# List-scheduled attention-and-GLU block: a longer assumed latency for DMA transposes, an earlier place for the gate-times-up products, a slack for TensorE

## The chip, the core and the metric

One core of a Trainium2 chip. The metric is device time in microseconds (us). A run is called slow when it is over 1.5% above the fastest of its kernel; one run of the kernel before (249.89 us) is such a run and is left out.

## The reference

For 2048 tokens of width 512, in bfloat16:

```python
xn  = layernorm(x)
q, k, v = split(xn @ wqkv)                       # 32 heads of 16
phi(a)  = concat(softmax(a @ w_phi), softmax(-(a @ w_phi)))
kv, z   = sum_s phi(k) v, sum_s phi(k)           # per head
A   = (phi(q) kv / (phi(q) z + 1e-6)) @ wo       # linear attention
B   = (gelu(xn @ w_gate) * (xn @ w_up)) @ w_down # width 1376
out = x + A + B
```

## The kernel before

The kernel records every operation with the buffers that it reads and writes, its engine, an assumed cost and (for a DMA) an assumed latency. A list scheduler then simulates the engines with these numbers and so fixes the order of instructions on each. The numbers reach the chip in no other way: **they only decide the order** and, for a few copies that two engines can do, the engine. Each engine is given its instructions in that order, with semaphore waits between them.

```python
def schedule(self):
    ...
    h = min((x for x in cand[n] if x.ready <= t + 1e-9), key=lambda x: x.prio)
    ...
    free[n] = t + h.cost
    h.end = t + h.cost + h.lat
    if h.kb:
        h.end = moved = max(moved, t + h.lat) + h.kb / 345
    for u in h.users:
        slack = self.slack if u.eng == "pe" and n != "pe" else 0.0   # self.slack = 0.0
        u.ready = max(u.ready, ... h.end + slack)
```

The work falls into four stages: a start (layer norm of the first four 128-token tiles, their transposes on TensorE, the first gate matmuls); the gate/up matmuls of the first 512 tokens (L550) with the weight folding; the key, query and value projections (L443, L498); and from about 76 us a long mixed stage. In that stage every attention tile t goes through this chain across engines:

```python
def q_prep(t):                       # POOL sums, VectorE normalises Eq, then two DMA transposes
    ...
    for h in range(2):
        dma("sp", lambda e, h=h: e.dma_start_transpose(EqT[:, t % NQT, 4*h:4*h+4, :], E[...]),
            reads=B_Eq[t], writes=[B_EqT[t % NQT][h]], cost=1.2, lat=1.4, kb=310)

def att(t):                          # TensorE: 2 x 4 small matmuls (L573), VectorE: divide
    ...
    dma("sp", lambda e: e.dma_start_transpose(oT[:, t % NOT, :, :], o_sb[:, k, :]),
        reads=[B_o[k]], writes=[B_oT[t % NOT]], cost=1.2, lat=1.4, kb=310)

def outp(t, b, direct):              # TensorE: 4 matmuls with oT (L594), 11 with hT (L598)
    ...

def ffn(J):                          # 4 gate matmuls, 4 up matmuls (L550), in banks J%2 and 2+J%2
    lin(wg_sb, ...); lin(wu_sb, ...)
    return glu(J, gb, ub)            # ScalarE gelu(gate) -> gs, VectorE hT = gs * up
```

All transposes and all output stores are issued from one queue, SyncE, in order. Gate and up matmuls are the filling with which TensorE covers the chain's latencies. Two PSUM banks each hold gates and ups, so filling is limited by how soon gelu and product free them.

The softmax here doesn't subtract the row's maximum and nothing guards it: scores larger than these inputs give would overflow.

## Time and profile before

| | before |
|---|---|
| median time | 195.86 us (fast runs 195.78 to 195.86) |
| span in the profile | 194.0 us |
| TensorE busy | 187.2 us, 96% |
| VectorE / POOL / ScalarE busy | 64% / 56% / 44% |

The page of the kernel before: busy time per engine, TensorE's share of each fortieth of the span in tenths, and the chain that ended last by engine and line.

```profile
span 194.0 us, 3172 instructions
PE 187.2 (96%) x1175; PEld 95.5 (49%) x1196; DVE 123.6 (64%) x227; ACT 85.3 (44%) x147; POOL 108.3 (56%) x151
...
PE   7999999999999999999899999999999999999993
...
PE 89%; DMA 6%; DVE 2%; issue 1%; ACTq 0%; SPq 0%
```

A digit 9 is 90% or more. TensorE is full except for the first slice, the last, and one dent near the middle. (1175 matmul records beside 1196 weight loads show that 21 matmul records are missing.)

The waits of TensorE in the kernel before: who waited for whom, us in total, times, longest.

```profile
PE ps_all L656 <- DVE warm L390: 1.2, 1, 1.2
PE ps_all L594 <- DMA oT<-o_sb: 0.9, 1, 0.9
PE ps_all L565 <- DMA wg_sb<-in_B_w_gate_dram: 0.3, 1, 0.3
PE ps_all L573 <- DMA EqT<-Eq: 0.2, 1, 0.2
```

The dent itself, from TensorE's timeline of the kernel before. The columns are start, length, what, how many, and in brackets the idle time before it.

```profile
90.47 0.29 PE L573 MATMUL ps_all<-kvr,EqT 128*128 128x68 bf16 x4
90.94 0.30 PE L573 MATMUL ps_all<-kvr,EqT 128*128 128x68 bf16 x4 [0.17 <-DMA EqT<-Eq]
91.07 1.02 PE L550 MATMUL ps_all<-xnT,wu_sb 128*128 128x512 bf16 x4
91.94 1.03 PE L550 MATMUL ps_all<-xnT,wg_sb 128*96 128x512 bf16 x4
92.80 0.42 PE L573 MATMUL ps_all<-kvr,EqT 128*128 128x68 bf16 x8
94.14 1.04 PE L594 MATMUL ps_all<-wo_sb,oT 128*128 128x512 bf16 x4 [0.93 <-DMA oT<-o_sb]
```

The same stretch in the chain of waits of the kernel before shows the two landings (start, us, what):

```profile
86.48 4.41 DMA EqT<-Eq
...
91.63 2.47 DMA oT<-o_sb
```

### The profile page before, as it was taken

How to read it: one execution, taken by the hardware profiler on the slowest of the kernel's cores; microseconds unless marked ns; L12 is line 12 of the kernel's file. 1: busy time of each engine (PE TensorE's matmuls, PEld its weight loads, DVE VectorE, ACT ScalarE, POOL GpSimd, SP SyncE). 2: the span in 40 equal slices, each digit the busy share in tenths (PEclk: the TensorE clock that was granted, in tenths of full speed). 3: DMA queues.
4: the chain of work that ended last, by engine and by line, in shares of the span. 5: the costliest groups of instructions: out<-in, count | busy, mean ns of one | idle time of the engine just before them, and what ended most of it. 6: DMA issues, size and time to landing. Idle time of an engine off the chain costs nothing.

```text
span 194.0 us, 3172 instructions
## 1 busy us (share of the span) xinstructions
PE 187.2 (96%) x1175; PEld 95.5 (49%) x1196; DVE 123.6 (64%) x227; ACT 85.3 (44%) x147; POOL 108.3 (56%) x151
## 2 busy tenths in 40 slices
PE   7999999999999999999899999999999999999993
PEld 2665565444545554454444444444544444454452
DVE  4699895489877675995948987659445361431121
ACT  2382798998797888423040041322223222231000
POOL 6630202799999999999449999979502202021000
PEclk9999999999999999999999999999999999999999
DMA  5999944456020000017456446535442221210101
GB/s 138 349 397 381 189 86 54 83 146 254 3 54 0 3 0 0 0 27 82 91 101 136 84 111 124 107 74 121 92 108 56 55 54 27 54 30 27 54 27 54
DMA packets 41630, 18.60 MB, mean 96 GB/s; under 512 B 33312, under 2 KB 41136, under 8 KB 41616
## 3 DMA queue, kind: packets, MB, share of 16 engines
q1 hardware_dynamic: 40496, 15.94, 35.3%
q0 software_dynamic: 560, 1.95, 3.0%
q10 hardware_dynamic: 560, 0.52, 0.8%
q8 instruction: 9, 0.15, 0.3%
q14 instruction: 5, 0.04, 0.1%
HBM read 8.44 MB, written 2.10 MB: 54 GB/s over the span
## 4 chain that ended last, share of the span: by engine, by line
PE 89%; DMA 6%; DVE 2%; issue 1%; ACTq 0%; SPq 0%
PE ps_all L550 33%; PE ps_all L598 19%; PE ps_all L443 14%; PE ps_all L498 7%; PE ps_all L594 6%; DMA wg_sb<-in_B_w_gate_dram 3%; DMA EqT<-Eq 2%; PE ps_all L565 2%; PE ps_all L573 2%; PE ps_all L518 2%; DMA oT<-o_sb 1%; PE ps_all L624 1%; PE ps_all L636 1%; PE ps_all L647 1%; DVE Eq L480 1%
## 5 line engine op out<-in xcount | busy, mean ns | idle before, releaser
L550 PE MATMUL ps_all<-xnT,wu_sb 128*128 128x512 bf16 (+1 forms) x172 | 43.8, 379 | 0.3
L543 DVE TENSOR_TENSOR hT<-gs,ps_all 128x512 bf16<-128x512 bf16 (+1 forms) x44 | 29.4, 680 | 22.1 <-PE ps_all L550 21.4
L473 POOL TENSOR_TENSOR st<-st 128x256 f32<-128x256 f32 (+1 forms) x54 | 38.9, 720 | 3.7
L541 ACT ACTIVATE gs<-ps_all 128x512 bf16<-128x512 f32 (+1 forms) x44 | 25.8, 597 | 32.6 <-PE ps_all L550 29.6
L550 PE MATMUL ps_all<-xnT,wg_sb 128*128 128x512 bf16 (+1 forms) x154 | 39.8, 379 | 0.3
L598 PE MATMUL ps_all<-wd_sb,hT 128*128 128x512 bf16 (+1 forms) x164 | 38.0, 379 | 0.2
L610 POOL TENSOR_TENSOR ob<-y_sb,x_all 128x512 bf16<-128x512 f32 x12 | 14.7, 1228 | 41.1 <-ACT y_sb L608 41.0
L608 ACT ACTIVATE y_sb<-ps_all 128x512 f32<-128x512 f32 x12 | 7.2, 597 | 45.4 <-PE ps_all L598 40.5
L550 PEld LDWEIGHTS ps_all<-xnT,wu_sb 128*128 128x128 bf16 (+1 forms) x176 | 17.3, 100 | 19.3
L598 PEld LDWEIGHTS ps_all<-wd_sb,hT 128*128 128x128 bf16 (+1 forms) x165 | 16.1, 98 | 19.5
L550 PEld LDWEIGHTS ps_all<-xnT,wg_sb 128*128 128x128 bf16 (+1 forms) x160 | 14.9, 100 | 14.4
L447 ACT ACTIVATE Ek<-ps_all 128x512 bf16<-128x512 f32 x32 | 17.3, 622 | 4.4 <-PE ps_all L443 4.1
L447 ACT ACTIVATE Eq<-ps_all 128x512 bf16<-128x512 f32 x32 | 18.3, 631 | 1.0 <-PE ps_all L443 0.8
L473 POOL TENSOR_TENSOR st<-Eq 128x512 f32<-128x512 bf16 x15 | 17.3, 1155 | 0.0
L473 POOL TENSOR_TENSOR st<-Ek 128x512 f32<-128x512 bf16 x12 | 14.4, 1197 | 3.7 <-ACT Ek L447 3.7
L498 PE MATMUL ps_all<-wv_sb,xnT 128*128 128x512 bf16 x63 | 16.2, 379 | 0.1
L443 PE MATMUL ps_all<-wk,xnT 128*128 128x512 bf16 x62 | 15.8, 379 | 0.1
L443 PE MATMUL ps_all<-wq,xnT 128*128 128x512 bf16 x61 | 15.8, 379 | 0.2
L594 PE MATMUL ps_all<-wo_sb,oT 128*128 128x512 bf16 x56 | 14.7, 379 | 1.0 <-DMA oT<-o_sb 0.9
L480 DVE TENSOR_TENSOR Ek<-Ek,rk 128x1024 bf16<-128x1024 bf16 x16 | 14.0, 875 | 0.5
L480 DVE TENSOR_TENSOR Eq<-Eq,rq 128x1024 bf16<-128x1024 bf16 x16 | 13.0, 812 | 0.4
L406 DVE BATCH_NORM_STATS2 stats<-x_all 128x6 f32<-128x512 bf16 x16 | 10.8, 674 | 1.1 <-DMA x_all<-in_A_x_dram 1.0
(73 smaller groups left out, 191.2 us busy)
## 6 DMA issues: line engine op xcount, KB each, us to landing
out_dram<-ob SPq DMA_DIRECT2D x15, 128.0 KB, 1.9
x_all<-in_A_x_dram SPq DMA_DIRECT2D x3, 512.0 KB, 9.0
wd_sb<-in_B_w_down_dram POOLq DMA_DIRECT2D x1, 1280.0 KB, 8.0
wg_sb<-in_B_w_gate_dram SPq DMA_DIRECT2D x2, 432.0 KB, 6.3
wu_sb<-in_B_w_up_dram SPq DMA_DIRECT2D x2, 432.0 KB, 7.3
wu_sb<-in_B_w_up_dram SPq DMA_DIRECT2D x2, 256.0 KB, 4.6
hT<-in_A_wqkv_dram SPq DMA_DIRECT2D x2, 256.0 KB, 8.2
Eq<-in_A_wqkv_dram SPq DMA_DIRECT2D x2, 256.0 KB, 9.0
```

The lines of the kernel that those rows point to most:

```text
L406: op("dve", lambda e: e.bn_stats(stats[:, t, :], x_all[:, t, :]), reads=[B_x[t]], writes=[B_stats[t]], cost=0.69, extra=extra)
L443: op("pe", [lambda e, i=i: e.matmul(bank(b), xnT[:, i, t * P:(t + 1) * P], w2[:, i, :], start=(i == 0), stop=(i == 3)) for i in range(4)], ...
L447: exps.append(op("act", lambda e, sig=sig: e.activation(E[:, t, :, sig, :], bank(b).rearrange("p (b c) -> p b c", c=64), ACTF.Exp, scale=( ...
L473: op("pool", lambda e, o=o, a=a, n=n: e.tensor_tensor(o, a[:, :, 0:n], a[:, :, n:2 * n], op=ALU.add), reads=ba, writes=bo, cost=c, lock=k < 3)
L480: op("dve", lambda e: e.tensor_tensor(ev, ev, r, op=ALU.mult), reads=[Br], writes=BE, cost=0.92, lock=True)
L498: op("pe", [lambda e, i=i: e.matmul(bank(b), xnT[:, i, t * P:(t + 1) * P], wv_sb[:, i, :], start=(i == 0), stop=(i == 3)) for i in range(4 ...
L541: h = op("act", lambda e: e.activation(gs[0:w, k, :], bank(gb)[0:w, :], ACTF.Gelu_apprx_tanh), reads=[BK[gb]], writes=[B_gs[k]], cost=0.55 ...
L543: op("dve", lambda e: e.tensor_tensor(hT[0:w, s % 2, jf, :], gs[0:w, k, :], bank(ub)[0:w, :], op=ALU.mult), reads=[B_gs[k], BK[ub]], write ...
L550: op("pe", [lambda e, i=i: e.matmul(bank(b)[0:w, :], wt[:, i, jf * 128:jf * 128 + w], xnT[:, i, s * 512:(s + 1) * 512], start=(i == 0), st ...
L594: fns = [lambda e, j=j: e.matmul(bank(b), oT[:, t % NOT, j, :], wo_sb[:, j, :], start=(j == 0), stop=False) for j in range(4)]
L598: fns.append(lambda e, jf=jf, w=w: e.matmul(bank(b), hT[0:w, s % 2, jf, tl * 128:(tl + 1) * 128], wd_sb[0:w, jf, :], start=False, stop=(jf ...
L610: op("pool", lambda e: e.tensor_tensor(ob[:, k, :], y_sb[:, y, :], x_all[:, t, :], op=ALU.add), reads=[B_y[y], B_x[t]], writes=[B_ob[k]], ...
```

## The change

The intent is to let the scheduler place uses of transposed tiles later, so that TensorE does other work meanwhile. No operation is added or removed. A transpose's assumed latency goes from 1.4 to 4.0 (attention and output tiles) or 1.8 (the normalised input), its assumed cost from 1.2 to 1.33. The products are put 60 places forward in priority. Every result of another engine is assumed to reach TensorE 0.2 us later.

```diff
@@ xt_dma @@
-  reads=[B_xn[k]], writes=[B_xnT[t]], cost=1.2, lat=1.4, kb=310)
+  reads=[B_xn[k]], writes=[B_xnT[t]], cost=1.33, lat=1.8, kb=310)
@@ q_prep @@
-  reads=B_Eq[t], writes=[B_EqT[t % NQT][h]], cost=1.2, lat=1.4, kb=310)
+  reads=B_Eq[t], writes=[B_EqT[t % NQT][h]], cost=1.33, lat=LT, kb=310)
@@ glu @@
-  reads=[B_gs[k], BK[ub]], writes=[B_hT[s % 2][jf]], cost=0.69)
+  reads=[B_gs[k], BK[ub]], writes=[B_hT[s % 2][jf]], cost=0.69, prio=len(S.ops) - 60)
@@ att @@
-  reads=[B_o[k]], writes=[B_oT[t % NOT]], cost=1.2, lat=1.4, kb=310)
+  reads=[B_o[k]], writes=[B_oT[t % NOT]], cost=1.33, lat=LT, kb=310)
@@ main @@
+  LT = 4.0
+  S.slack = 0.2
   S.schedule()
```

What this does to TensorE's order around the dent (g and u are gate and up matmuls, A attention, O the oT matmuls of an output tile, d its hT matmuls, each with its count):

```
before:  ... g8 A8 g8 A8       u4 g4 A8 O4 d11 O4 d11 ...
after:   ... g8 A8 u8 g8 A4 g4 A4 u4 g8 O4 d11 A8 ...
```

## The prediction

> **What bounds the kernel now.** TensorE. The page gives PE 187.2 us busy of a 194.0 us span at granted clock 1.0, and the chain of waits is 89% PE. The table by stretches shows PE over 98% busy from 8 to 91 us and from 98 us on; VectorE (64%), POOL (56%) and ScalarE (44%) have room. The first 7.2 us wait for the gate weights; the last 3 us are the last eviction and store. Useful PE work runs from 7.28 to about 191.1 us with one notable hole. The Trainium skill ("Perfetto Trace Analysis", Identifying the Most-Contended Engine) warns that matmul busy time does not measure nearness to the peak; I use it only to find holes, and take matmul time from starts (four 128x512 matmuls every 0.86 us).
>
> **The hole, 90.5 to 94.2 us.** The chain: VectorE normalises attention tile 1 (Eq), its transpose, issued at 86.48, lands at 90.89 (4.41 us), the second half of attention 1 waits 0.17 us; attention 0's output transpose (oT) lands at 94.10, after 2.47 us, and the output product waits 0.93 us for it. The schedule had assumed 1.4 us. The skill (same page, DMA Instruction - HWDGE) says that the profiled span of an issue does not contain the data movement; the trace agrees: issue 1.26 us, landing 2.4 to 4.5 us.
>
> **What the change does.** No instruction is added or removed, only the order on each engine moves, as the comparison of the orders shows:
> - Attention 0 stays behind the same PE work. But between it and the first half of attention 1 there are now 16 gate/up matmuls (3.45 us) instead of 8, and between attention 0 and the first output product 32 instead of 16: 3.4 us more cover, against a shortage of 0.93 us. Both waits (1.1 us) should vanish. The gate-times-up products come earlier on VectorE, which frees the PSUM banks and gelu buffers that this extra PE work needs; adding VectorE durations (0.6 us each) by hand, I find no bank late.
> - At the start the second PE transpose moves ahead of the gate weights' landing, into time that PE waited anyway (0.22 us), and the 0.19 us wait for a copy of xnT should go, as eight more gate matmuls cover it. Gain 0.2 to 0.4 us.
> - The down-weight loads are issued slightly later, long before use. POOL's sums (about 3.3 us a tile) run ahead of PE's use. The tail is the same. Nothing there.
>
> **Sum.** 1.1 + 0.3 = 1.4 us, all on the critical path, less 0.1 us for some new small wait: 195.86 - 1.3 = 194.5 us. Range 193.9 to 195.8. Faster by over 2% (below 191.9) would need 3.9 us of PE holes, and there are not that many: 1%. Within 2%: 97%. Slower by over 2%: 2%.
>
> **What would show it.** PE busy unchanged within 0.5 us; no PE wait for oT or EqT in the waits; the 91 to 98 us stretch as full as its neighbours; the chain no longer through EqT or oT; the first 128x512 up product 0.2 to 0.4 us earlier than 11.7; span about 192.7. VectorE, ACT and POOL busy unchanged, only moved.
>
> **What would make it wrong.** A new PE wait for a bank: gates run up to three groups ahead of their ups at 88 to 96 us, so a late gelu or product (VectorE 93% busy there) would stall PE. A transpose stuck on the SyncE queue behind a store that waits for POOL. Weight loads at the start: if the second part of the gate/up weights lands just as PE needs it, an earlier start is handed back as a wait. Missing matmul records could hide small waits.

## The result

| | before | after |
|---|---|---|
| median time, us | 195.90 (fast 195.78 to 195.93) | 194.29 (193.86 to 194.48, 4 runs) |
| span in the profile, us | 194.0 | 192.5 |
| ratio of the fast runs | | 0.9917, 95% interval 0.9896 to 0.9938 |

A ratio is the mean time of one kernel's fast runs over that of the other's of the same rounds, so it is not quite the ratio of the medians quoted. The gain of 1.6 us is clear of noise and lies in the predicted range.

The page of the changed kernel, the lines that answer to those above:

```profile
span 192.5 us, 3190 instructions
PE 188.1 (98%) x1196; PEld 95.2 (49%) x1196; DVE 127.8 (66%) x228; ACT 85.1 (44%) x146; POOL 106.6 (55%) x151
...
PE   7999999999999999999999999999999999999993
...
PE 95%; DVE 1%; DMA 1%; POOL 0%; issue 0%
```

The dent is gone, and the chain holds almost nothing but TensorE. Its busy time rose by 0.9 us because no matmul record is missing here: the kernel before, profiled once more with all 1196 records (b_again, below), shows 188.2 us.

TensorE's waits in the changed kernel; this is the whole list:

```profile
PE ps_all L657 <- DVE warm L390: 1.2, 1, 1.2
```

The stretch of the dent in TensorE's timeline of the changed kernel:

```profile
90.42 1.89 PE L550 MATMUL ps_all<-xnT,wg_sb 128*128 128x512 bf16 x8
92.15 0.29 PE L573 MATMUL ps_all<-kvr,EqT 128*128 128x68 bf16 x4
92.28 1.04 PE L550 MATMUL ps_all<-xnT,wg_sb 128*96 128x512 bf16 x4
93.15 0.29 PE L573 MATMUL ps_all<-kvr,EqT 128*128 128x68 bf16 x4
93.28 1.02 PE L550 MATMUL ps_all<-xnT,wu_sb 128*128 128x512 bf16 x4
94.14 1.89 PE L550 MATMUL ps_all<-xnT,wg_sb 128*128 128x512 bf16 x8
95.87 1.03 PE L594 MATMUL ps_all<-wo_sb,oT 128*128 128x512 bf16 x4
```

Every start now follows the one before by the count times 0.216 us (or 0.032 us for attention). The first output product starts 1.73 us later than before and finds nothing to wait for.

Two things changed at this place, though, not one. Besides the later use, the first oT is issued sooner, as it no longer stands behind tile 2 in the queue:

```profile
90.23 1.19 SPq L589 DMA_TRANSPOSE oT<-o_sb  x1
```

VectorE finished its data at 90.20, so the issue waited 0.03 us (before: 1.38). Counted from the start of attention 0, oT lands after 4.24 us (before: 5.61) and is used after 7.43. The old order, without its losses, would use it after 4.22 (5.65 - 1.43). So either the queue's new order or the added cover could remove nearly all of oT's wait; the experiments below have to be read with this in mind.

### A budget for all profiles

The experiments are judged on four distances between matmul starts in the trace. They are exact to some 0.05 us and free of the jitter of launch and first loads: (a) start of the first gate matmul, (b) from there to the first key projection, (c) from there to attention 0, (d) from attention 0 to the last matmul.

| profile | a | b | c | d |
|---|---|---|---|---|
| before | 7.28 | 23.55 | 57.66 | 102.23 |
| before, again, other chip | 7.34 | 23.55 | 57.66 | 102.26 |
| **after** | 7.45 | 23.32 | 57.66 | 100.79 |
| after, again, other chip | 7.70 | 23.32 | 57.66 | 100.79 |
| b_pad64 | 7.58 | 23.55 | 57.66 | 101.28 |
| b_pad32 | 7.25 | 23.55 | 57.66 | 101.45 |
| b_pad256 | 7.10 | 23.71 | 57.91 | 101.64 |
| a_pad216 | 7.15 | 23.34 | 57.66 | 100.79 |
| lat_only | 7.73 | 23.55 | 57.66 | 101.23 |
| slack_only | 7.94 | 23.32 | 57.66 | 102.55 |
| no_lat | 7.55 | 23.32 | 57.66 | 102.62 |
| no_prio | 7.49 | 23.32 | 57.66 | 101.42 |
| no_slack | 7.00 | 23.55 | 56.80 | 101.65 |
| a_wgfirst | 7.43 | 23.33 | 57.66 | 100.79 |

So after against before is +0.17 (a), -0.23 (b), 0.00 (c), -1.44 (d): the 1.50 us between the spans. Column a is noise of the first loads: it ranges from 7.0 to 7.9 us, and in most profiles the matmul waits for the gate weights. In no_slack attention 0 stands one group of matmuls earlier, so there c and d must be added.

### The profile page after: what moved, and what is told of

It reads as the page before. It is cut to its first block, busy times and chain, and to the rows that moved or that the text cites. A ratio compares the mean times of both kernels' runs of the same rounds, so it can differ in the third digit from the quotient of the medians.

```text
span 192.5 us, 3190 instructions
## 1 busy us (share of the span) xinstructions
PE 188.1 (98%) x1196; PEld 95.2 (49%) x1196; DVE 127.8 (66%) x228; ACT 85.1 (44%) x146; POOL 106.6 (55%) x151
## 4 chain that ended last, share of the span: by engine, by line
PE 95%; DVE 1%; DMA 1%; POOL 0%; issue 0%
PE ps_all L550 38%; PE ps_all L598 19%; PE ps_all L443 14%; PE ps_all L498 7%; PE ps_all L594 7%; PE ps_all L518 2%; PE ps_all L573 2%; PE ps_all L565 2%; DMA x_all<-in_A_x_dram 1%; PE ps_all L624 1%; PE ps_all L647 1%; PE ps_all L636 1%; DVE stats L406 1%; PE ps_all L619 0%; PE ps_all L435 0%; DVE xn_sb L421 0%
## 5 line engine op out<-in xcount | busy, mean ns | idle before, releaser
L550 PE MATMUL ps_all<-xnT,wg_sb 128*128 128x512 bf16 (+1 forms) x160 | 40.4, 379 | 0.0
L610 POOL TENSOR_TENSOR ob<-y_sb,x_all 128x512 bf16<-128x512 f32 x12 | 13.9, 1160 | 41.3 <-ACT y_sb L608 41.2
L473 POOL TENSOR_TENSOR st<-Eq 128x512 f32<-128x512 bf16 x15 | 17.9, 1190 | 0.0
L443 PE MATMUL ps_all<-wq,xnT 128*128 128x512 bf16 x64 | 16.4, 379 | 0.0
L480 DVE TENSOR_TENSOR Ek<-Ek,rk 128x1024 bf16<-128x1024 bf16 x16 | 15.7, 983 | 0.5
L594 PE MATMUL ps_all<-wo_sb,oT 128*128 128x512 bf16 x60 | 15.4, 379 | 0.0
L480 DVE TENSOR_TENSOR Eq<-Eq,rq 128x1024 bf16<-128x1024 bf16 x16 | 14.7, 919 | 0.5
L412 POOL TENSOR_SCALAR vpe<-mv 128x1 f32<-128x1 f32 (+1 forms) x7 | 1.6, 227 | 19.6 <-DVE mv L408 19.6
```

The costliest lines, as they stand in the source:

```text
L443: op("pe", [lambda e, i=i: e.matmul(bank(b), xnT[:, i, t * P:(t + 1) * P], w2[:, i, :], start=(i == 0), stop=(i == 3)) for i in range(4)], ...
L473: op("pool", lambda e, o=o, a=a, n=n: e.tensor_tensor(o, a[:, :, 0:n], a[:, :, n:2 * n], op=ALU.add), reads=ba, writes=bo, cost=c, lock=k < 3)
L480: op("dve", lambda e: e.tensor_tensor(ev, ev, r, op=ALU.mult), reads=[Br], writes=BE, cost=0.92, lock=True)
L550: op("pe", [lambda e, i=i: e.matmul(bank(b)[0:w, :], wt[:, i, jf * 128:jf * 128 + w], xnT[:, i, s * 512:(s + 1) * 512], start=(i == 0), st ...
L594: fns = [lambda e, j=j: e.matmul(bank(b), oT[:, t % NOT, j, :], wo_sb[:, j, :], start=(j == 0), stop=False) for j in range(4)]
L610: op("pool", lambda e: e.tensor_tensor(ob[:, k, :], y_sb[:, y, :], x_all[:, t, :], op=ALU.add), reads=[B_y[y], B_x[t]], writes=[B_ob[k]], ...
```

## The experiments

### Why was oT late? A look that changed the theory

The prediction had blamed an assumed latency of 1.4 us against a landing of 2.47. But the scheduler adds kb/345, so it assumed 1.4 + 310/345 = 2.3 us, nearly the ordinary landing. Something else made oT late. In the kernel before, VectorE finished attention 0's output at 90.25, while its transpose was issued only at 91.63. These are lines of VectorE's and of SyncE's timelines (for a DMA the length is that of the issue, not of the landing):

```profile
89.56 0.69 DVE L585 TENSOR_TENSOR o_sb<-ps_all,rden 128x512 bf16<-128x512 f32 x1
...
87.79 2.48 SPq L492 DMA_TRANSPOSE EqT<-Eq  x1
...
91.63 1.26 SPq L589 DMA_TRANSPOSE oT<-o_sb  x1
```

An issue usually takes 1.19 to 1.27 us here; this one, of a tile needed later, took 2.48 and stood ahead of oT in the queue. What happened to the DMA at that time, in the DMA view from 87.7 to 89.3 us of the kernel before (the busy share of the 16 DMA engines in 40 slices, then each queue with packets, MB and share)?

```profile
DMA  9368999999999989939990090000000000000010
...
q8 instruction: 1, 0.02, 5.8%
```

One packet of an instruction queue, 16,384 bytes, ran from 87.72 to 89.21 us (its record in the trace). The transposes' own packets stop meanwhile, at about 88.5 us. Tile 1's second transpose, then in flight, landed after 4.41 us. The Trainium skill ("Runtime: NRT & Kernel Launch", Instruction fetch mechanics) says that each sequencer fetches its instructions over a DMA queue in blocks of 16 KiB, 256 instructions, and that the cost of crossing a block is "mostly hidden". The traces agree with the first: such a packet comes every 14 to 23 us in the two kernels, after some 210 to 290 weight loads and matmuls, so it is TensorE's stream (an inference from the count; the padding below moves the packets and so confirms it). For TensorE itself they agree with the second too: in the changed kernel's first profile it lost nothing at any of nine fetches. What the section does not speak of is other transfers. The 14 profiles hold 672 attention and output transposes. Four of them (slack_only and no_prio, tile 0, issued at 43 to 45 us) ran beside the loads of the down weights, landed after 5.6 to 6.6 us, long before their use, and are set aside. Of the other 668, 99 landed after more than 2.7 us (up to 4.5), and **all 99 overlapped a packet of an instruction queue** (86 one of 16 KB, 13 one of 8 KB of another instruction queue). Only 17 overlapped a 16 KB packet and still landed on time; of those that met only an 8 KB packet, 40 did. Undisturbed, a landing takes 2.48 us (2.38 to 2.56).

That is a correlation. The first experiments move the fetch.

### Moving the fetch: b_pad64, b_pad32, b_pad256, a_pad216

Edit: waits that are already satisfied, put into TensorE's stream among the matmuls of the weight folding and the projections (22 to 67 us). The order of everything else is as it was. (Lines of the kernel shift by 3 in these runs.)

```diff
-    for waits, fns, inc in S.out[name]:
+    for j, (waits, fns, inc) in enumerate(S.out[name]):
+        if name == "pe" and 40 <= j < 72:          # b_pad64; others: 56, 104 or 94 with 4 or 8 waits
+            for _ in range(4):                     # two of these make one instruction
+                eng.wait_ge(S.eng_sems["dve"], 1)
         for sem, val in waits:
```

**b_pad64** (kernel before, 64 instructions more). Expected:

> The kernel before, unchanged in every order, with 64 extra instructions in TensorE's stream (waits already satisfied) among the projection matmuls, so that the 16 KB instruction fetch that ran at 87.7 to 89.2 us comes about 64 instructions, near 4.9 us, earlier, before the transposes of attention tile 1. Theory A (the hole at 90 to 94 us is this fetch delaying one transpose to 4.4 us and holding the SyncE queue): tile 1's transposes land in about 2.5 us, PE has no wait for oT or EqT, 194.5 us. Rival B (an ordinary landing of 2.5 us is already longer than the cover in the old order): the 1.4 us hole stays, 195.9 us.

Measured: 194.62 us, ratio 0.9954 (0.9925 to 0.9983). The fetch came at 82.2 us. The transposes of tile 1 landed in the ordinary time (the last line for EqT, issues between 85.5 and 87.5 us):

```profile
DMA to landing us min/median/max: 2.4/2.5/2.5
```

The loss in the dent fell from 1.43 to 0.18 us, with TensorE's order unchanged: oT was issued 0.17 us after its data and landed 4.39 us after attention 0 began. A fetch at 104.6 us made another oT late, and TensorE lost 0.25 us at 107 us. Column d is 0.95 us better than before; the changed kernel's is 1.44 us better. Rival B, ordinary latency, is out.

**b_pad32.** Expected:

> As b_pad64 with 32 extra instructions: the fetch moves about 2.4 us earlier, to near 85.3 us, where it can still touch tile 1's first transpose. Theory A: the hole is smaller or gone, 194.4 to 195.6 us, and the time follows whether a transpose of tile 1 lands late. Rival B: 195.9 us.

Measured: 195.17 us, ratio 0.9978 (0.9949 to 1.0008), so in time alone not told from before. The trace tells more: the fetch came at 83.2 us, tile 1 landed on time, the dent lost 0.18 us, and at 107 us 0.43 us was lost to an oT that met the next fetch. Column d gained 0.78.

**b_pad256**, meant as a control. Expected:

> Control: the kernel before with 256 extra satisfied waits, one whole 16 KB block, so that a fetch falls near 87.7 us again. Theory A: hole and time as before, 195.9 us within 0.4. If the extra instructions themselves cost or save time, it shows here.

Measured: 195.75 us, ratio 1.0023 (0.9979 to 1.0068). As a control it failed: the fetch came at 85.1 us, not 87.7, and tile 1 landed on time. The dent lost 0.33 us, 107 us lost 0.49 us, and the extra instructions themselves cost about 0.4 us in columns b and c. It shows that padding is not free, and that a fetch can't be placed to better than some 3 us.

**a_pad216** (changed kernel). Expected:

> The changed kernel with 216 extra satisfied waits, so that a fetch which ran at 84.7 us falls near 88 us instead, on the transposes of tile 1, as in the kernel before. Theory A with cover (the changed order has 3.4 us more PE work before the use): a late landing of about 4.4 us shows in the trace and PE still does not wait, 194.3 us within 0.3. Rival C (the changed kernel gained only because its fetch happened to come 3 us earlier): a hole of about 1 us returns, 195.2 us or more.

Measured: 194.17 us, ratio to before 0.9935 (0.9907 to 0.9963). Here the fetch did come at 88.1 us, on tile 1's second transpose (the same line, issues at 84.9 and 86.1 us; 4.3 is that one):

```profile
DMA to landing us min/median/max: 2.4/3.3/4.3
```

TensorE lost nothing after the start; column d is 100.79, as in the changed kernel. Rival C, that the changed kernel was merely lucky with its fetch, is out. But the run does not show the cover at work on oT. The stalled transpose had nothing behind it in the queue: oT was issued 0.03 us after its data and landed 4.24 us after attention 0. Only the transpose of tile 1 came late, 2.21 us after attention 0, where the old order would use it at 2.11. An estimate from these landings: the old order of TensorE would have lost some 0.2 us here, not 1.43. The changed kernel run once more (a_again, below) also had this collision (fetch at 88.0, landing 4.25 us) and also lost nothing.

### The kernel before, again

Edit: none. Expected:

> The kernel before once more, unchanged, on another chip: does the collision repeat? Theory A expects the same place for the fetch that ran at 87.7 us, within about 1.5 us, since it depends on the instruction stream; if it comes there, the second transpose of attention tile 1 lands after 4 us or more and PE loses about 1.4 us between 90 and 94 us; if it comes 3 us earlier by chance, that transpose lands in 2.5 us and the loss is under 0.3 us. Rival B (ordinary latency) expects the 1.4 us loss in either case. Time ratio 1.00.

Measured: 196.06 us, ratio 1.0009. The fetch came at 87.8 us, tile 1's second transpose landed after 4.16 us, and the dent lost 1.18 us; another 0.25 us went at 108 us. Column d is 102.26. The collision belongs to this program, not to one run.

### Parts of the change: lat_only, slack_only, no_lat, no_prio, no_slack

Each takes parts of the diff above and leaves out the rest. The new numbers of the input transposes (1.33 and 1.8) were kept in no_lat, no_prio and no_slack; they were not tried alone.

**lat_only.** Expected:

> Only the larger latency of the attention and output transposes (4.0 instead of 1.4), no priority, no slack, no change to the first transposes. Its order has 12 gate/up matmuls between attention 0 and the first half of attention 1, and 28 before the first output product (before: 8 and 16; changed kernel: 16 and 32). Theory A: no PE wait for oT or EqT; from attention 0 to the last matmul 100.8 us as in the changed kernel; the start is as before (0.2 us worse than changed): ratio 0.993, 194.5 us. Rival D (the priority of the products is what makes it): holes of 0.5 us or more remain, ratio 0.996 or more.

Measured: 195.23 us, ratio 0.9959 (0.9920 to 0.9998). No wait for oT or EqT, although the fetch met tile 1 (4.33 us). But there is a new wait, seen in TensorE's timeline:

```profile
91.35 0.82 PE L550 MATMUL ps_all<-xnT,wu_sb 128*128 128x512 bf16 x3 [0.27 <-DVE hT L543]
```

An up matmul waits for its bank, which VectorE's product has not yet freed: 0.43 us lost by starts, exactly column d's excess over the changed kernel (101.23 - 100.79). So the latency alone was worth 1.0 us. My expectation of 100.8 had missed this.

**no_prio.** Expected:

> The changed kernel without the earlier priority of the gate-times-up products (latency, slack and the first transposes' numbers kept). Theory: latency gives the cover and priority keeps the extra up matmuls from waiting for a bank, as the latency alone lost 0.43 us at 90.7 us to a product: start 23.3 us; a PE wait of 0.2 to 0.6 us for a product near 91 us, no wait for oT or EqT: attention 0 to last 101.0 to 101.4 us; ratio 0.994 to 0.996. If priority is needless: 100.8 us, ratio 0.992.

Measured: 195.04 us, ratio 0.9967 (0.9936 to 0.9999). The same 0.43 us wait for a product near 91 us, and another 0.18 us behind attention tile 1 at 92.9 us. The priority therefore saves about 0.4 to 0.6 us, and it is needed because the new order asks for banks sooner: without the latency it gains nothing (no_lat).

**slack_only.** Expected:

> Only the 0.2 us slack of TensorE for other engines' results. Its order keeps 8 and 16 matmuls at attention 1 and the first output product, but has the changed kernel's start. Theory A: from the first gate matmul to the first key projection 23.3 us (before 23.55); the hole at 90 to 94 us stays up to 1.4 us, as the fetch falls; ratio 0.997 to 1.000.

Measured: 196.29 us, ratio 1.0015 (0.9975 to 1.0055). Column b gained 0.23 us as expected. The dent stayed, 1.22 us, and another 0.53 us went at 108.6 us, where a fetch had met an oT (landing 3.75 us). The dent is a warning to my theory: no transpose of tiles 1 and 2 landed late here. SyncE's timeline shows why it is there all the same:

```profile
86.52 5.28 SPq L492 DMA_TRANSPOSE EqT<-Eq  x4
91.84 1.26 SPq L589 DMA_TRANSPOSE oT<-o_sb  x1
```

Four ordinary issues of 1.3 us, begun 1.27 us later than in the kernel before (0.43 us of that because attention 0 and all before it ran later, the rest because a product that stands before them on VectorE waited for its up matmuls, which TensorE did one group of four later), fill the queue until 91.8. oT's data were ready at 90.68. So the fetch is only one way to the dent. The common cause is **oT standing behind two transposes of a later tile in the in-order SyncE queue**, with 4.2 us of TensorE's work as cover. A stalled issue or a late first issue is enough to use it up.

**no_lat.** Expected:

> The changed kernel without the larger latency (priority, slack and the first transposes' numbers kept). Its order has 12 matmuls before attention 1 and 20 before the first output product, 4.8 us of cover. Theory A: the start gains 0.2 us; the later part loses 0 to 0.8 us in waits for oT or EqT, as the fetch falls: att. 0 to last 100.8 to 101.7 us; ratio 0.992 to 0.998. Rival D (priority does it all): no wait at all, ratio as the changed kernel, 0.992.

Measured: 196.21 us, ratio 1.0006 (0.9957 to 1.0056): no gain at all, and a larger loss than I had allowed for. The dent at 90 to 94 us is gone, although the fetch met tile 1 (4.19 us): here too the first oT stands before tile 2 in the queue, lands 4.22 us after attention 0 and is used at 4.83. So the queue's order with only 0.6 us more cover is enough for this dent. But a new one opens at the fourth output tile:

```profile
108.28 0.39 PE L594 MATMUL ps_all<-wo_sb,oT 128*128 128x512 bf16 x1 [1.66 <-DMA oT<-o_sb]
```

Its oT data were ready at 101.86 and issued at 104.52, after two transposes of EqT and an output store in the queue; a fetch at 105.4 us then stretched the landing to 3.72 us. Column d lost 1.83 us. Without the larger latency the priority (with the slack and the input transposes' numbers) only moves the dent. Rival D is out.

**no_slack.** Expected:

> The changed kernel without the 0.2 us slack. Theory: the slack is worth the start alone: first gate to first key projection 23.55 us (changed 23.32), attention 0 to last 100.8 us and no PE wait for oT, EqT or a product; 0.2 us slower than the changed kernel: ratio 0.993.

Measured: 194.41 us, ratio 0.9938 (0.9902 to 0.9974); the changed kernel in the same rounds 194.28. Column b is 23.55, b + c + d is 0.23 us over the changed kernel's, and nothing waits later. The slack is worth the start alone: the scheduler puts the second TensorE transpose before the gate matmuls, into time when TensorE waits for the gate weights anyway.

### The changed kernel again, and an attempt at its start

**a_again.** Expected:

> The changed kernel once more on the chip of these runs, as their base: 23.3 us from the first gate matmul to the first key projection, 57.66 to attention 0, 100.8 from there to the last matmul, no PE wait for oT or EqT though some transposes land after 4 us: ratio to before 0.992.

Measured: 194.28 us, ratio 0.9928 (0.9902 to 0.9953), columns b, c and d as in the first profile.

**a_wgfirst.** With nothing lost after the first gate matmul, only the start is left. Edit:

```diff
+load_f(wg_sb, B_w_gate, 0, B_wg)
 load_x("sp", 2, 1)
 load_x("act", 3, 1)
-load_f(wg_sb, B_w_gate, 0, B_wg)
```

Expected:

> The changed kernel with the first gate weights loaded ahead of the third and fourth tile of x (three lines moved); orders of all engines but the two loads unchanged. In ten profiles the gate weights landed at 6.3 to 7.9 us and the first gate matmul waited for them until 7.1 to 7.9 us. Expected: weights land before 6.8 us, the first gate matmul starts at 7.1 to 7.2 us, held by the copy of xnT instead; everything after is as in the changed kernel: 0.3 us faster than it (0.0 to 0.6). It fails if the third tile of x then lands too late for its transpose near 8.4 us.

Measured: 194.37 us against 194.28 for the changed kernel in the same rounds: no gain, a miss. The weights landed at 5.6 us instead of 7.6, and TensorE's wait for them is gone. But in its timeline the first gate matmul now stands behind the second transpose, which was held up until 7.19:

```profile
7.19 0.40 PE L435 MATMUL ps_all<-ident,xn_sb 128*128 128x128 bf16 x4
7.43 0.78 PE L565 MATMUL ps_all<-xnT,wg_sb 128*128 128x128 bf16 x11
```

The chain through layer norm ends almost when the weights did. No version run here beats the changed kernel by more than the noise.

## Why the prediction was right, and where its reasoning was not

- *"Both waits (1.1 us) should vanish"* by more TensorE work between attention 0 and its uses. Right in outcome: in the four profiles of this order a transpose landed after 4.0 to 4.4 us and TensorE lost nothing. The mechanism is only half shown. The prediction left oT's landing where it was and put 3.4 us of work before its use; in fact oT also landed 1.1 to 1.4 us earlier (4.24 to 4.25 us after attention 0 instead of 5.37 and 5.61), as the new schedule changed the SyncE queue, and that alone covers nearly all of the shortage. By arithmetic the cover alone would do as well (5.61 against 7.43), but in no run of this order did the first oT land late, so no run separates the two. The size was too small: 1.44 us in column d. I had summed bracketed idle times, which count from a modelled end. The Trainium skill says so ("Perfetto Trace Analysis", Summary: the profiler window per engine type: TensorE's reported end is estimated); here it hid 0.33 of 1.43 us.
- *"Gain 0.2 to 0.4 us"* at the start. The order gained 0.23 us: the moved transpose, 0.22 us. The wait of 0.19 us for a copy of xnT did not go. It stayed at 0.18 us and only moved to the last group of gate matmuls. And in the profiled run the weights landed 0.17 us later, so the whole start looks 0.06 us better.
- *"Less 0.1 us for some new small wait"*: none came. *"I find no bank late"*: right, and no_prio and lat_only show that it holds only with the priority.
- Sum: 1.3 us predicted; the medians differ by 1.61 us, the spans by 1.50.
- *"The schedule had assumed 1.4 us"*: wrong. It assumed 2.3 us with the size term, close to the ordinary 2.48. oT was late because its issue stood 1.38 us in the SyncE queue behind a later tile, and in the kernel before because a fetch held that issue. I had named the queue only as a risk for the new order; it was the cause in the old one.
- *"VectorE ... busy unchanged, only moved"*: wrong by 4.2 us. Of this, 0.7 us is the copy that came from ScalarE, and 3.4 us are the same 32 normalising multiplications, which took longer. Lines of VectorE's groups, before and after (busy us, mean ns of one):

```profile
L480 DVE TENSOR_TENSOR Ek<-Ek,rk 128x1024 bf16<-128x1024 bf16 x16 | 14.0, 875 | 0.5
```

```profile
L480 DVE TENSOR_TENSOR Ek<-Ek,rk 128x1024 bf16<-128x1024 bf16 x16 | 15.7, 983 | 0.5
```

  One takes 0.69 us when no POOL operation runs beside it, and mostly 1.0 to 1.6 us when POOL's first sum does. The skill ("SBUF — State Buffer", Who interferes with whom) says that a VectorE instruction with two inputs in SBUF contends with a GpSimd instruction that reads SBUF; both are of this kind, and the trace agrees. TensorE lost nothing after the start, so it cost nothing.

What stays open: why a fetch of 0.9 to 1.6 us delays a transpose by up to 2 us. A DMA is complete only when all the DMA engines that it uses have reported (the skill, "DMA: Bandwidth & Descriptors", Why a DMA increments its semaphore by 16 and not by 1), so one engine held by a fetch would hold the whole transpose. The trace has no engine for a packet, so this is argued, not shown. It fits what moved between the fetch's end and 90.2 us in the kernel before, when tile 1's transpose was still not down: a thin stream, about one engine's share of 16 (the DMA view from 89.2 to 90.2 us; packets, MB and share).

```profile
q1 hardware_dynamic: 42, 0.01, 7.8%
```

The new latency of the input transposes was not tried alone; columns b and c show no effect of it.

## What to carry to other kernels

When an in-order engine is the bottleneck, schedule each use of a DMA result for its late landing, not its median: here 4.4 us, not 2.5. Cover costs nothing as long as there is other work and its buffers are free, and the priority on the products was needed for exactly that. Before believing a latency, look at when the data were ready, when the issue began, and what stood ahead of it in the same queue. In an in-order queue, issue first what is needed first: with the fetch in the same place, oT landed 4.25 us after attention 0 in the new queue and 5.37 in the old (a_again, b_again). And measure a hole by the distance between starts.

## What the Trainium skill lacked or had wrong

- "Runtime: NRT & Kernel Launch", Instruction fetch mechanics: calls the cost of crossing a 16 KiB block mostly hidden and says nothing of other transfers. Here all 99 of 668 DMA transposes that landed after more than 2.7 us (up to 4.5, ordinary 2.48) overlapped an instruction fetch, and an issue then took up to 2.7 us instead of 1.2 to 1.3. In the kernel before this was part of a 1.43 us hole on the bottleneck.
- "DMA: Bandwidth & Descriptors", DMA Transpose (X-bar): gives no time for one small transpose inside SBUF; "VectorE: DVE Perf Modes" (The three transpose paths) has one for 128x128 alone, 1309 ns. Here 128x512 in bfloat16 took 1.19 to 1.27 us to issue and 2.4 to 2.55 us to land, and issues from one queue follow each other every 1.3 us.
- "Advanced Engine Details and Errata", VectorE Performance Modes: names only VectorE instructions in a two-port mode as blocking with GpSimd, and its table gives tensor_tensor no such mode. Here tensor_tensor multiplications of 0.69 us mostly took 1.0 to 1.6 us beside POOL's first sum. The page "SBUF — State Buffer" has the case, without a figure for it.
- "Perfetto Trace Analysis", Summary: says that a matmul's end is estimated, not what follows. Here two waits of 0.17 and 0.93 us by the modelled ends were 0.34 and 1.09 us by starts.
